# A linear attention with a gated FFN on one core: the last result tiles go to dead operand buffers, and the whole instruction order is rewritten

## The chip, the core and the metric

The kernel runs on one core of a Trainium2 chip. The metric is device time of one execution in microseconds; the kernel before was run three times, with a median of 962.52 us (962.49 to 966.88). One further execution was recorded by the hardware profiler. TensorE does the matrix products, VectorE (DVE) and GpSimd (POOL) do element-wise work, ScalarE (ACT) does activations, copies and some of the DMA issues, and SyncE (SP) issues nearly all other DMAs.

## The reference, cut to what matters

```python
# q, k, v: (8 batches, 8 heads, 576, 64) float32; moe weights float64; 4608 tokens, d_model 512, d_ff 1536
q_s = softmax(q, over the 64 features);  k_s = softmax(k, over the 576 positions)
kv  = einsum('bhsd,bhse->bhde', k_s, v)
x   = einsum('bhsd,bhde->bhse', q_s, kv)          # then 8 heads side by side: 4608 x 512
xn  = x / sqrt(mean(x * x, over the 512) + 1e-6) * rms_g
g   = xn @ w_gate;  val = xn @ w_val              # 512 x 1536 each
out = (g * sigmoid(g) * val) @ w_out              # 1536 x 512, result 4608 x 512 float32
```

## The kernel before

**Data.** The three weights arrive as 8-byte words. `load_w` (L444) brings raw words in by SP, and four steps turn them into float32: `conv_low` (L451) and `conv_mul` (L457) on ACT, `conv_shift` (L460) on DVE, `conv_add` (L465) on POOL. Every matrix operand is then split into a high and a low part, and each product is three matmuls: high by high, high by low, low by high.

**Stages.** Tokens are worked in 9 blocks of 512. The attention part of a block loads q, k and v pieces (SP), takes the maxima and sums of the softmax (DVE), and makes x. Blocks 0 to 2 run the FFN plainly in 12 steps each: `f1` (L973) makes the gate and value products in PSUM, `g_mul` (L978, DVE) scales the gate, `silu` (L982, ACT), `h_mul` (L985, DVE) multiplies, `h_hi` (L408, ACT) and `h_lo` (L994, POOL or DVE) split, and `f2` (L1010) multiplies by w_out. While these run, combinations of the weights are made and kept in DRAM. Blocks 3 to 8 run as three pairs, p = 0, 1, 2. Their first product is a Strassen-Winograd scheme with 7 instead of 8 block products (`pp`, L1122), whose weights come back from DRAM through POOL's queue (`w_in`, L1095, tiles `ring` and `w`); sums of the products are `c_...` (L1143, DVE), and `hm` (L1185, DVE or POOL) multiplies gate and value. The second product is plain for pair 0 and by the same scheme for pairs 1 and 2: `qq` (L1331) multiplies, with weights that SP loads (`qw`), operand parts from `qb_hi` (L408) and `qb_lo` (L1316), and sums on DVE (`q_comb`, L1340) that leave four quadrants, 11, 12, 21 and 22, each in two halves x = 0 and 1.

**The end of the last pair.** For each of these eight halves `qtr` (L1357 to L1360) transposes 32 x 32 pieces on DVE into an `ot` tile, of which there are two (`bufs=2`). For the last pair `qput` (SP) stores the first two 32-row groups of it, and `qpua` (ACT) the other two, each 64 KB by one DMA at L1368. An `ot` tile can be written again when all four stores from it are in. The weights' tiles `w_0` to `w_5`, taken over by the Strassen operands in `operand()` (L1035), are not used again once the last pair's first product is done.

**What sets the order.** Every instruction's place is set by a table, the string `ORDER` (L22): 3345 steps, each the name of a function with its numbers, and after a colon the engine where there is a choice (A, D or P). A loop at L1385 calls them in that order, and each engine executes its own instructions strictly in it. A DMA that SP or ACT issues takes one of eight completion counters in turn, shared by both queues, and its issue waits until the one before it on that counter is in.

Of the kernel before, what the change touches and what calls it, by code (L numbers as in the profile page):

```python
# [8 lines left out]
F32 = mybir.dt.float32  # L9
# [13 lines left out]
exp_table k_load.0.0 q_load0.0.0 kv_zero.4 kv_zero.5 v_ones.0.0 kv_zero.0 k_load.0.2 kv_zero.7 q_load0.0.3 constants  # L23
v_ones.0.1 kv_zero.3 warm.2.3 kv_zero.6 k_max0.0.0 q_load0.0.2 v_ones.0.2 kv_zero0.0 warm.2.10 kv_zero0.1 q_max0.0.0
k_load.0.1 warm.2.1 q_load0.0.1 q_sub0.0.0:P warm.2.6 load_w.0.1 v_ones.0.3 k_max0.0.2 k_load.0.3 q_exp.0.0 warm.2.12
v_load.0.0 k_tr.0.0 warm.2.13 k_top.0.0 q_max0.0.2 k_rows.0.0 load_w.0.2 warm.2.8 k_max0.0.1 k_tr.0.2 warm.2.9
v_load.0.1 q_sub0.0.2:P k_sub.0.0 k_tr.0.1 warm.2.11 warm.2.5 g_load q_max0.0.3 q_exp.0.2 warm.2.7 load_w.0.0 k_top.0.1
q_sub0.0.3:P k_exp.0.0 q_sum0.0.0 k_rows.0.1 warm.9 q_max0.0.1 v_load.0.2 q_exp.0.3 q_eps0.0.0 k_top.0.2 q_sub0.0.1:P
q_rec0.0.0 k_sub.0.1 k_load.1.0 q_mul0.0.0:P q_sum0.0.3 q_exp.0.1 k_exp.0.1 q_sum0.0.1 q_t0.0.0 k_max0.0.3 k_rows.0.2
conv_low.0.2.1 v_load.0.3 k_mm.0.0 conv_low.0.1.1 k_sub.0.2 warm.2.4 q_c0.0.0:A load_w.1.1 k_tr.0.3 warm.2.0  # L30
conv_mul.0.1 q_eps0.0.1 k_eps.0.0 q_eps0.0.3 k_mm.0.1 q_rec0.0.1 k_top.0.3 k_exp.0.2 q_mul0.0.1:P k_rec.0.0 q_sum0.0.2
load_w.1.0 k_rows.0.3 kv_norm0.0.0:A conv_shift.0.1 conv_mul.0.0 q_x0.0.0 q_eps0.0.2 q_rec0.0.3 conv_add.0.1.1
k_eps.0.1 k_sub.0.3 conv_low.0.0.1 q_load0.1.0 q_t0.0.1 conv_mul.0.2 conv_shift.0.0 k_mm.0.2 q_mul0.0.3:P x_hi.0.0:A
k_rec.0.1 conv_shift.0.2 q_c0.0.1:A conv_add.0.0.1 q_rec0.0.2 kv_norm0.0.1:A k_eps.0.2 k_max.1.0 k_exp.0.3 q_x0.0.1
load_w.2.1 q_mul0.0.2:P x_sq.0.0 k_rec.0.2 x_lo.0.0 k_mm.0.3 q_load0.1.1 x_sq.0.1 kv_norm0.0.2:D v_ones.1.0
conv_add.0.2.1 w_hi.0.0.2:A k_tr.1.0 q_t0.0.2 k_eps.0.3 k_top.1.0 k_rec.0.3 x_hi.0.1:D k_rows.1.0 conv_mul.1.1 q_t0.0.3
w_lo.0.0:P warm.2.2 q_c0.0.2:A conv_shift.1.1 kv_norm0.0.3:A q_x0.0.2 x_lo.0.1 kv_zero.2 q_c0.0.3:A load_w.2.0
w_lo.0.1:P k_sub.1.0 conv_mul.1.0 load_w.1.2 q_x0.0.3 x_sq.0.2 v_load.1.0 conv_shift.1.0 n_sum0.0 x_hi.0.2:A q_max0.1.0
x_hi.0.3:A n_sum0.1 x_lo.0.2 q_sub0.1.0:P x_sq.0.3 x_lo.0.3 o_hi.0:A n_sum0.2 q_exp.1.0 q_max0.1.1 o_lo.0:P n_sum0.3
conv_mul.2.1 q_sum0.1.0 conv_low.1.0.2 f1.0.0.0.0 load_w.2.2 conv_shift.2.1 q_sub0.1.1:P f1.0.0.0.1 f1.0.0.0.2  # L40
load_w.4.1 n_t.0 f1.0.0.0.3 conv_mul.2.0 f1.0.1.0.0 load_w.3.1 f1.0.0.1.0 conv_add.1.0.2 f1.0.1.0.1 k_exp.1.0
load_w.4.0 n_y0.0 f1.0.1.0.2 f1.0.1.0.3 conv_shift.2.0 f1.0.0.1.1 conv_low.2.0.2 f1.0.0.1.2 f1.0.0.1.3 n_y1.0
f1.0.1.1.0 load_w.3.0 f1.0.1.1.1 q_exp.1.1 f1.0.1.1.2 f1.0.1.1.3 conv_add.2.0.2 f1.0.0.2.0 w_hi.1.0.2:A f1.0.0.2.1
f1.0.0.2.2 f1.0.0.2.3 q_load0.1.2 k_mm.1.0 n_rows.0 conv_mul.1.2 conv_low.1.2.1 f1.0.1.2.0 g_mul.0 f1.0.1.2.1
f1.0.1.2.2 f1.0.1.2.3 q_eps0.1.0 silu.0 k_eps.1.0 q_rec0.1.0 k_rec.1.0 w_lo.1.0:D f1.1.0 conv_shift.1.2 q_mul0.1.0:P
load_w.6.0 conv_mul.4.1 k_load.1.2 h_mul.0 w_lo.1.1:P w_hi.2.0.2:A kv_norm0.1.0:D f1.1.1 conv_shift.4.1 conv_add.1.2.1
h_hi.0:A load_w.5.0 g_mul.1 conv_mul.4.0 k_load.1.1 conv_mul.3.1 h_lo.0:D o_hi.1:A w_lo.2.0:P conv_shift.4.0 silu.1
f2.0 conv_shift.3.1 load_w.6.1 conv_low.4.0.2 load_w.5.1 h_mul.1 w_lo.2.1:P q_max0.1.2 conv_low.2.2.1 conv_mul.2.2
o_lo.1:D load_w.4.2 conv_mul.3.0 f1.2.0 q_sub0.1.2:P conv_shift.2.2 conv_shift.3.0 conv_mul.6.0 conv_add.4.0.2
load_w.3.2 conv_low.3.0.2 conv_shift.6.0 k_max.1.2 q_load.2.0 q_t0.1.0 f1.2.1 g_mul.2 q_c0.1.0:A conv_add.3.0.2  # L50
q_exp.1.2 k_max.1.1 h_hi.1:A q_sum0.1.2 q_x0.1.0 w_hi.4.0.2:A q_eps0.1.2 h_lo.1:D k_tr.1.1 f2.1 x_hi.1.0:A load_w.5.2
w_lo.4.0:D w_hi.3.0.2:A load_w.8.0 k_top.1.1 q_sum0.1.1 load_w.7.0 silu.2 x_lo.1.0 w_lo.3.1:P load_w.7.1 f1.3.1
v_ones.1.1 q_eps0.1.1 conv_add.2.2.1 q_rec0.1.2 q_rec0.1.1 v_load.1.1 conv_low.6.0.2 h_mul.2 w_lo.3.0:D x_sq.1.0
o_hi.2:A q_mul0.1.2:D k_rows.1.1 conv_mul.6.1 f1.3.0 o_lo.2:P k_sub.1.1 h_hi.2:A conv_shift.6.1 conv_mul.5.0 kv_zero.1
h_lo.2:D conv_low.3.2.1 load_w.6.2 conv_shift.5.0 conv_add.6.0.2 conv_mul.5.1 q_load0.1.3 f2.2 g_mul.3 conv_mul.3.2
conv_shift.5.1 silu.3 conv_shift.3.2 conv_low.4.2.1 q_mul0.1.1:P h_mul.3 conv_mul.7.0 conv_mul.4.2 f1.4.0
conv_shift.7.0 conv_add.3.2.1 h_hi.3:A conv_shift.4.2 conv_low.5.0.2 v_ones.1.2 w_lo.4.1:D load_w.7.2 v_load.1.2
h_lo.3:D o_hi.3:A o_lo.3:P q_t0.1.1 g_mul.4 f1.4.1 q_c0.1.1:A conv_mul.5.2 conv_add.5.0.2 conv_mul.7.1 conv_shift.5.2
silu.4 q_max.2.0 k_exp.1.1 conv_shift.7.1 q_load.2.1 k_tr.1.2 f2.3 conv_add.4.2.1 q_max0.1.3 q_half.2.0 w_hi.5.0.2:A
h_mul.4 k_top.1.2 w_hi.6.0.2:A w_lo.5.1:D k_mm.1.1 w_lo.5.0:D h_hi.4:A k_rows.1.2 f1.5.0 k_eps.1.1 q_max2.2.0  # L60
conv_low.5.2.1 k_rec.1.1 q_sub.2.0:P kv_norm0.1.1:D o_hi.4:A load_w.10.0 load_w.8.1 w_lo.6.1:D q_exp.2.0 load_w.10.1
q_sub0.1.3:P k_sub.1.2 conv_low.7.0.2 load_w.8.2 q_x0.1.1 k_load.1.3 q_sum.2.0 h_lo.4:P k_exp.1.2 g_mul.5 f1.5.1
conv_low.6.2.1 o_lo.4:D x_hi.1.1:A w_lo.6.0:P x_sq.1.1 x_lo.1.1 q_exp.1.3 q_half2.2.0 silu.5 conv_add.7.0.2 k_mm.1.2
q_sum0.1.3 f2.4 k_eps.1.2 conv_mul.7.2 h_mul.5 conv_low.7.2.1 v_ones.1.3 conv_shift.7.2 conv_add.5.2.1 load_w.9.1
h_hi.5:A kv_hi.1.0:D conv_mul.8.1 k_rec.1.2 kv_norm0.1.2:D f1.6.0 conv_add.7.2.1 w_hi.7.0.2:A conv_shift.8.1 o_hi.5:A
q_eps0.1.3 load_w.9.2 conv_low.8.0.2 q_rec0.1.3 h_lo.5:D load_w.9.0 load_w.10.2 w_lo.7.1:D q_t0.1.2 o_lo.5:D f1.6.1
q_c0.1.2:A o_hi.7:D conv_mul.6.2 w_lo.7.0:D conv_low.10.0.2 g_mul.6 o_lo.7:P q_max.2.1 conv_mul.8.2 conv_shift.6.2 f2.5
x_acc.1.1:P silu.6 conv_shift.8.2 conv_mul.8.0 h_mul.6 conv_add.6.2.1 conv_low.8.2.1 conv_shift.8.0 conv_mul.9.0
h_hi.6:A k_max.1.3 conv_add.8.2.1 f1.7.0 conv_mul.9.1 conv_low.9.2.1 q_sum2.2.0 v_ones.2.0 conv_shift.9.0
conv_add.8.0.2 load_w.11.2 o_hi.6:A v_load.1.3 conv_shift.9.1 conv_low.9.0.2 q_rec.2.0 f1.7.1 o_lo.6:D w_hi.8.0.2:A  # L70
h_lo.6:P g_mul.7 w_lo.8.0:D k_tr.1.3 q_x0.1.2 load_w.11.0 conv_add.9.0.2 k_top.1.3 load_w.11.1 q_half.2.1 f2.6
k_load.2.0 x_hi.1.2:A x_sq.1.2 x_lo.1.2 silu.7 conv_mul.10.1 w_lo.8.1:P h_mul.7 k_rows.1.3 h_hi.7:A f1.8.0 q_mul0.1.3:P
k_sub.1.3 w_hi.9.0.2:A q_mul.2.0:D o_hi.8:A q_load.2.2 h_lo.7:P conv_shift.10.1 conv_mul.10.2 conv_mul.10.0 f1.8.1
w_lo.9.0:D k_exp.1.3 w_lo.9.1:P conv_shift.10.2 conv_shift.10.0 g_mul.8 o_lo.8:P conv_mul.9.2 f2.7 conv_low.10.2.1
conv_shift.9.2 v_load.2.0 silu.8 conv_add.10.0.2 n_cols.0 conv_mul.11.0 f1.9.0 conv_add.9.2.1 conv_shift.11.0 q_t.2.0
h_mul.8 kv_hi.1.2:D h_hi.8:A q_t0.1.3 o_hi.9:A k_mm.1.3 h_lo.8:D w_hi.10.0.2:A g_mul.9 o_lo.9:P f1.9.1 k_load.2.1
k_eps.1.3 silu.9 k_rec.1.3 q_c0.1.3:D w_lo.10.0:P kv_hi.1.1:A kv_norm0.1.3:D conv_low.11.2.1 q_load.2.3 conv_mul.11.2
kv_hi.1.3:D x_acc.1.2:P conv_mul.11.1 f1.10.0 conv_shift.11.2 conv_shift.11.1 kv_lo.1.1:P q_max.2.2 conv_add.10.2.1
q_max2.2.1 h_mul.9 q_half.2.2 v_ones.2.1 q_x0.1.3 w_lo.10.1:P f2.8 v_load.2.1 h_hi.9:D g_mul.10 h_lo.9:D silu.10
k_max.2.0 x_sq.1.3 x_hi.1.3:A f1.10.1 o_hi.10:A kv_lo.1.0:D x_acc.1.3:D conv_low.11.0.2 o_lo.10:D conv_add.11.0.2 f2.9  # L80
# [264 lines left out]
def linear_attention_then_gated_ffn(ctx: ExitStack, tc, q, k, v, w_gate, w_val, w_out, rms_g, out):  # L345
    nc = tc.nc
    B, H, S, D = q.shape
    NT, DM = out.shape
# [1004 lines left out]

    def q12(p, x):
        q_comb(p, x, 12, ux[p, "q", x, 2], 2, 2)

    def qtr(p, n, x):  # L1357
        src = qacc[p, 0, x] if n == 11 else ux[p, "q", x, n]
        t = ux[p, "o", x, n] = fp.tile([P, DM], F32, name="ot", bufs=2)
        nc.vector.transpose(t, src)  # L1360
# [57 lines left out]
```

## Time and profile before

| what | before |
|---|---|
| median of 3 runs | 962.52 us (962.49 to 966.88) |
| the profiled execution | 971.66 us, of which its span is 969.9 us |
| TensorE matmul busy | 927.0 us, 96% of the span |
| VectorE busy | 745.6 us, 77% |
| GpSimd busy | 525.1 us, 54% |
| ScalarE busy | 474.7 us, 49% |
| the last matmul ends | 949.71 us after the span's start |

The span is the time from the first to the last instruction that the profiler saw; the execution has 1.8 us around it. In the rows below a time in brackets says how long the engine sat idle before the instruction, and behind the arrow stands what it waited for. PE is TensorE's matrix products, SPq and ACTq are the DMA queues of those engines, and PEclk is the granted TensorE clock as a share of full speed.

### The profile page before, as it was taken

To read this page: it belongs to the slowest core of one execution; us is meant where nothing else is said; L and a number is where in the kernel's file an instruction comes from. 1 tells how busy PE (TensorE), PEld (TensorE's weight loads), DVE (VectorE), ACT (ScalarE), POOL (GpSimd) and SP (SyncE) were. 2 spreads that over 40 slices of the span, in tenths; PEclk is the share of its full clock that TensorE was granted. 3 is DMA by queue.
4 is the path that set the end of the run, shared out by engine and by line. 5 is a ranking of instruction groups with operands and counts; after the bars stand their busy time and mean duration, and the time that the engine had idled before them with its cause. 6 is when DMAs were issued, how large, how long until landed. Compare 5 with 4: busy or idle time off the path is not lost.

```text
span 969.9 us, 14401 instructions
## 1 busy us (share of the span) xinstructions
PE 927.0 (96%) x4625; PEld 750.0 (77%) x4625; DVE 745.6 (77%) x1548; ACT 474.7 (49%) x742; POOL 525.1 (54%) x517
## 2 busy tenths in 40 slices
PE   6999999999999899999999999999999999999991
PEld 4688887777877687887887888888887888888881
DVE  6798868989887789888886698866569855545981
ACT  3999747687577475665534464321216311112320
POOL 4777959767588587774765545333232652412230
PEclk9899999999999999999999999999999999999996
DMA  9997425988976987899788698898538688684334
GB/s 207 279 269 231 137 79 197 303 278 287 320 219 192 254 242 195 207 231 242 197 218 260 220 267 270 272 283 288 169 130 298 155 233 251 216 258 130 109 82 60
DMA packets 215464, 211.80 MB, mean 218 GB/s; under 512 B 139828, under 2 KB 176732, under 8 KB 210780
## 3 DMA queue, kind: packets, MB, share of 16 engines
q1 hardware_dynamic: 190620, 121.73, 45.6%
q0 software_dynamic: 16320, 88.09, 28.8%
q10 hardware_dynamic: 8448, 1.05, 0.7%
q8 instruction: 37, 0.61, 0.3%
q14 instruction: 39, 0.32, 0.1%
HBM read 160.49 MB, written 50.33 MB: 217 GB/s over the span
## 4 chain that ended last, share of the span: by engine, by line
PE 82%; DMA 6%; SPq 5%; DVE 3%; ACT 2%; issue 1%; POOL 0%; ACTq 0%; DVEq 0%; POOLq 0%
PE ps_gv L1122 16%; PE ps_gv L973 15%; PE ps_o L1122 12%; PE ps_o L1010 7%; PE ps_a L1122 7%; PE ps_o L1331 6%; PE ps_a L1331 3%; PE ps_o L1215 3%; PE ps_gv L1331 3%; DMA qt<-in_q_dram 2%; PE ps_a L1215 2%; PE ps_gv L1215 2%; PE ps_a L577 2%; SPq L647 1%; PE ps_a L785 1%; DMA od<-o 1%
## 5 line engine op out<-in xcount | busy, mean ns | idle before, releaser
L973 PE MATMUL ps_gv<-xh,w 128*128 128x512 f32 x576 | 191.8, 400 | 6.3 <-DVE gs L978 5.0
L1122 PE MATMUL ps_gv<-x,ring 128*128 128x512 f32 x576 | 142.7, 392 | 0.0
L973 PEld LDWEIGHTS ps_gv<-xh,w 128*128 128x128 f32 x576 | 108.8, 189 | 32.5 <-DVE gs L978 5.8
L1122 PEld LDWEIGHTS ps_gv<-x,ring 128*128 128x128 f32 x576 | 107.1, 188 | 22.8 <-DVE tmp L1143 0.3
L973 PE MATMUL ps_gv<-xl,w 128*128 128x512 f32 x288 | 112.1, 393 | 0.0
L1143 DVE TENSOR_TENSOR tmp<-tmp,ps_gv 128x512 f32<-128x512 f32 x84 | 57.3, 685 | 41.4 <-PE ps_gv L1122 40.5
L1122 PE MATMUL ps_o<-x,ring 128*128 128x512 f32 x360 | 85.0, 389 | 0.0
L1095 POOL DMA_DIRECT2D ring<-wd x54 | 30.9, 573 | 93.4 <-PE ps_gv L1122 43.2
L1122 PEld LDWEIGHTS ps_o<-x,ring 128*128 128x128 f32 x360 | 67.5, 188 | 14.3 <-DVE tmp L1143 0.2
L1010 PE MATMUL ps_o<-o,hh 128*128 128x512 f32 x288 | 73.8, 398 | 2.5 <-ACT hh L408 2.5
L897 POOL TENSOR_TENSOR w<-w,w 128x512 fp32r<-128x512 f32 x43 | 61.0, 1426 | 11.5 <-ACT w L408 11.5
L1010 PEld LDWEIGHTS ps_o<-o,hh 128*128 128x128 f32 x288 | 52.8, 188 | 15.1 <-ACT hh L408 3.7
L973 PEld LDWEIGHTS ps_gv<-xl,w 128*128 128x128 f32 x288 | 54.4, 189 | 10.5 <-issue 0.2
L1143 DVE TENSOR_TENSOR tmp<-tmp,ps_o 128x512 f32<-128x512 f32 x42 | 28.7, 684 | 21.0 <-PE ps_o L1122 20.4
L1095 POOL DMA_DIRECT2D w<-wd x18 | 10.0, 556 | 58.3 <-PE ps_a L1122 29.1
L408 ACT CAST hh<-gs 128x512 fp32r<-128x512 f32 x48 | 29.5, 616 | 23.6 <-DVE gs L985 8.8
L534 DVE TENSOR_REDUCE cm<-kt 116x128 f32<-116x640 f32 x28 | 36.6, 1306 | 4.4 <-DMA kt<-in_k_dram 4.3
L1010 PE MATMUL ps_o<-o,hl 128*128 128x512 f32 x144 | 38.7, 391 | 0.0
L994 POOL TENSOR_TENSOR hl<-gs,hh 128x512 fp32r<-128x512 f32 x23 | 32.8, 1425 | 10.4 <-ACT hh L408 8.0
L1122 PE MATMUL ps_a<-x,ring 128*128 128x512 f32 x144 | 37.1, 393 | 0.1
L1122 PE MATMUL ps_a<-x,w 128*128 128x512 f32 x144 | 36.8, 391 | 0.0
L1122 PE MATMUL ps_gv<-x,w 128*128 128x512 f32 x144 | 35.5, 392 | 0.3 <-DVE w L1143 0.3
(620 smaller groups left out, 2312.1 us busy)
## 6 DMA issues: line engine op xcount, KB each, us to landing
ring<-wd POOLq DMA_DIRECT2D x36, 768.0 KB, 5.9
w<-wd POOLq DMA_DIRECT2D x24, 1024.0 KB, 6.0
ring<-wd POOLq DMA_DIRECT2D x18, 1024.0 KB, 6.0
wd<-w SPq DMA_DIRECT2D x12, 1024.0 KB
wd<-parts SPq DMA_DIRECT2D x24, 512.0 KB
o<-od POOLq DMA_DIRECT2D x18, 512.0 KB, 5.7
kt<-in_k_dram SPq DMA_DIRECT2D x28, 280.0 KB
vt<-in_v_dram SPq DMA_DIRECT2D x56, 140.0 KB
```

The lines of the kernel that those rows point to most:

```text
L408: (e.copy if e is nc.scalar else e.tensor_copy)(dst, src)
L534: nc.vector.tensor_reduce(out=cm, in_=kt_[b, g].rearrange("p h j d -> p h d j"), axis=AX.X, op=ALU.max)
L577: nc.tensor.matmul(pk[h * D:(h + 1) * D, :D + 1], lhsT=ke[:n, h, j], rhs=vt[:n, j, h], start=(j == 0), stop=(j == len(rows) - 1))
L897: on(nc.gpsimd).tensor_tensor(out=w[:, :, 1], in0=halves(s % NF, a, 1)[:, 0], in1=w[:, :, 0].bitcast(F32), op=ALU.subtract)
L973: nc.tensor.matmul(pd[s], lhsT=w[:, a, c // 2, m, c % 2 * P:c % 2 * P + P], rhs=X[j, c][x], start=(n == 1), stop=(n == 3 * NKT))
L994: on(nc.gpsimd).tensor_tensor(out=hl, in0=g_[s], in1=h_[s][0].bitcast(F32), op=ALU.subtract)
L1010: nc.tensor.matmul(po[t], lhsT=a[:, t * P:(t + 1) * P], rhs=w, start=(i == 0 and n == 0), stop=(i == NF - 1 and n == len(terms) - 1))
L1095: nc.gpsimd.dma_start(t, src.rearrange("p a b f -> p (a b f)"))
L1122: nc.tensor.matmul(abc[p, i, m, b], lhsT=src[:, h, c * P:(c + 1) * P], rhs=operand(o, c, x), start=first and n == 0, stop=n == 5, skip_gro ...
L1143: nc.vector.tensor_tensor(out=dst, in0=ux[u + (src,)], in1=abc[u + (b,)], op=ALU.add)
L1215: nc.tensor.matmul(pa[p, t, k], lhsT=a[:, k * P:(k + 1) * P], rhs=w, start=(c == 0 and n == 0), stop=(c == NF - 1 and n == 2))
L1331: nc.tensor.matmul(qacc[p, b, x], lhsT=ws[l][x], rhs=h[m], start=first and i == 0 and n == 0, stop=i == NH - 1 and n == 2, skip_group_chec ...
```

## The change

The last pair's transposed halves no longer go to the two `ot` tiles. Each half gets a slice of its own in two tiles that take the places `w_0` and `w_1`:

```diff
+    RES = {}
+
     def qtr(p, n, x):
         src = qacc[p, 0, x] if n == 11 else ux[p, "q", x, n]
-        t = ux[p, "o", x, n] = fp.tile([P, DM], F32, name="ot", bufs=2)
+        if p == NPAIR - 1:
+            m = (11, 22, 21, 12).index(n) * 2 + x
+            if m // 6 not in RES:
+                RES[m // 6] = big.tile([P, 6, TB], F32, name=f"res_{m // 6}", tag=f"w_{m // 6}")
+            t = RES[m // 6][:, m % 6]
+        else:
+            t = fp.tile([P, DM], F32, name="ot", bufs=2)
+        ux[p, "o", x, n] = t
         nc.vector.transpose(t, src)
```

And the whole of `ORDER` is another order of the same 3345 steps, with other engines for some of them. Its last lines before and after:

```diff
-... qq.2.3.5 qq.2.2.4.0 qq.2.2.5.0 qq.2.2.4.1 qq.2.2.5.1 qtr.2.11.1 q12.2.0 qput.2.11.1
-qpua.2.11.1 qput.2.21.0 qtr.2.12.0 qpua.2.12.0 qtr.2.11.0 q12.2.1 qput.2.11.0 qpua.2.11.0 ...
+qq.2.3.3 qb_lo.2.3.5:D qq.2.3.4.0 qq.2.3.5.0 qq.2.3.4.1 q12.2.0 qq.2.3.5.1 qtr.2.12.0 q12.2.1 qput.2.12.0 qpua.2.12.0
+qtr.2.12.1 qput.2.12.1 qpua.2.12.1
```

The numbers of matmuls (4249), of transposes (62) and of DMAs from SP (747) and POOL (108) stay. Two-input element-wise instructions go from 696 to 675 on DVE and from 348 to 369 on POOL; `hm` stands on POOL 30 times instead of 18. Table loads on ACT go from 58 to 52, and the step that loads the exponential's table at the very start now stands late in the order. Lines after the change are one higher near the top, and 10 higher behind `qtr`.

**The end, on DVE.** The last rows before; `tmp` and `gs` hold quadrant sums, `ps_o` and `ps_a` are PSUM banks, and a number tells tiles of one name apart.

```order
L1340 TENSOR_TENSOR tmp_4494<-tmp_4494,ps_o_8282 128x512
L1316 TENSOR_TENSOR hl_6794<-w_5834,hh_6793 128x512
L1316 TENSOR_TENSOR kv_102<-kt_7553,kv_102 128x512
L1360 STREAM_TRANSPOSE ot_9117<-ps_o_8203 128x512
L1340 TENSOR_TENSOR gs_8902<-gs_8902,ps_a_8817 128x512
L1360 STREAM_TRANSPOSE ot_9126<-gs_8902 128x512
L1360 STREAM_TRANSPOSE ot_9130<-ps_o_8202 128x512
L1340 TENSOR_TENSOR gs_8897<-gs_8897,ps_a_8818 128x512
L1360 STREAM_TRANSPOSE ot_9137<-gs_8897 128x512
L1360 STREAM_TRANSPOSE ot_9143<-tmp_4494 128x512
```

And the last rows after, with the tiles `res_0` and `res_1`.

```order
L1341 TENSOR_TENSOR tmp_4478<-tmp_4478,ps_o_8278 128x512
L1370 STREAM_TRANSPOSE res_0_9006<-tmp_4478 128x512
L1341 TENSOR_TENSOR tmp_4478<-tmp_4478,ps_o_8279 128x512
L1370 STREAM_TRANSPOSE res_0_9006<-tmp_4478 128x512
L1317 TENSOR_TENSOR vt_7112<-w_5828,kt_7111 128x512
L1317 TENSOR_TENSOR kv_102<-w_5828,kv_102 128x512
L1341 TENSOR_TENSOR gs_8902<-gs_8902,ps_a_8813 128x512
L1370 STREAM_TRANSPOSE res_1_9133<-gs_8902 128x512
L1341 TENSOR_TENSOR gs_8889<-gs_8889,ps_a_8814 128x512
L1370 STREAM_TRANSPOSE res_1_9133<-gs_8889 128x512
```

Five transposes stood behind the last operand part (L1316) and now two do; the other six halves are transposed before it.

**The first loads, on SP.** Before, from the third row of the queue (one k piece and two q halves stand ahead); `w_94` and `w_95` hold v and k pieces, `qt` and `r` q halves, `raw` weight words.

```order
L494 DMA w_95<-in_k_dram 96x2x384
L661 DMA r<-in_q_dram 128x256 x2
L661 DMA qt<-in_q_dram 128x256 x2
L494 DMA w_95<-in_k_dram 96x2x384
L661 DMA qt<-in_q_dram 128x256 x2
L444 DMA raw_98<-in_moe_w_val_dram 128x4x256
L494 DMA w_95<-in_k_dram 96x2x384
L519 DMA w_94<-in_v_dram 96x6x64 x2
L444 DMA raw_98<-in_moe_w_out_dram 128x1024
L519 DMA w_94<-in_v_dram 96x6x64 x2
L434 DMA g_sb<-in_moe_rms_g_dram 128x4x1
L444 DMA raw_98<-in_moe_w_gate_dram 128x4x256
```

After, from the start of the queue.

```order
L495 DMA w_95<-in_k_dram 96x2x384 x3
L662 DMA qt<-in_q_dram 128x256 x4
L495 DMA w_95<-in_k_dram 96x2x384
L662 DMA qt<-in_q_dram 128x256 x2
L445 DMA raw_99<-in_moe_w_val_dram 128x4x256
L445 DMA raw_98<-in_moe_w_val_dram 128x4x256
L520 DMA w_94<-in_v_dram 96x6x64 x2
L662 DMA r<-in_q_dram 128x256 x2
L445 DMA raw_98<-in_moe_w_gate_dram 128x4x256
L520 DMA w_94<-in_v_dram 96x6x64 x4
L520 DMA w_93<-in_v_dram 96x6x64 x2
L435 DMA g_sb<-in_moe_rms_g_dram 128x4x1
```

The first gate words stood behind one val tile, the w_out tile, two pairs of v pieces and the small `g_sb`; now they stand behind two val tiles and one pair of v pieces.

**Block 2's last steps, on DVE.** Before, the rows around the gate scaling of step 29 (`g_mul.29`, the L978 row): `st` tiles are the maxima of q pieces of block 5, `st_3745` from the piece whose load is `q_load.5.1`, `st_3752` from that of `q_load.5.0`.

```order
L713 TENSOR_REDUCE st_3745<-qt_3634 128x16
L718 TENSOR_REDUCE st_3745<-st_3745 32x16 x4
L713 TENSOR_REDUCE st_3752<-qt_3560 128x16
L718 TENSOR_REDUCE st_3752<-st_3752 32x16 x4
L726 TENSOR_REDUCE sw_3772<-st_3752 128x16
L597 TENSOR_SCALAR rs_3774<-ps_a_3758 128x1
L565 TENSOR_TENSOR kt_3290<-kt_3290,ps_a_3725 116x640
L978 TENSOR_TENSOR gs_3794<-ps_gv_3685,r_2777 128x512
```

After, the same place: `st_3756` is the maximum of the piece of `q_load.5.0`, `st_3776` that of `q_load.5.1`.

```order
L566 TENSOR_TENSOR kt_3502<-kt_3502,ps_a_3707 116x640
L714 TENSOR_REDUCE st_3756<-qt_3524 128x16
L979 TENSOR_TENSOR gs_3758<-ps_gv_3709,r_2897 128x512
L765 STREAM_TRANSPOSE qT_3761<-qt_3376 128x512
L714 TENSOR_REDUCE st_3776<-qt_3664 128x16
L775 TENSOR_TENSOR ql_3790<-qT_3647,qh_3684 128x512
```

Before, both maxima stood ahead of the gate scaling; after, only that of the earlier loaded piece does.

## Rows read from the trace of the kernel before

**Rows 1.** The page: span, TensorE's busy time, the chain by engine.
```profile
span 969.9 us, 14401 instructions
...
PE 927.0 (96%) x4625; PEld 750.0 (77%) x4625; DVE 745.6 (77%) x1548; ACT 474.7 (49%) x742; POOL 525.1 (54%) x517
...
PE 82%; DMA 6%; SPq 5%; DVE 3%; ACT 2%; issue 1%; POOL 0%; ACTq 0%; DVEq 0%; POOLq 0%
```

**Rows 2.** Timeline, 943 to 970 us: start, length, engine, line, operation [idle before].
```profile
948.85 0.86 PE L1331 MATMUL ps_o<-kv,x 128*128 128x512 f32 x3
949.75 0.72 DVE L1360 STREAM_TRANSPOSE ot<-ps_o 128x512 f32<-128x512 f32 x1 [4.33 <-PE ps_o L1331]
950.38 0.65 DVE L1340 TENSOR_TENSOR gs<-gs,ps_a 128x512 f32<-128x512 f32 x1
950.49 16.05 SPq L1368 DMA_DIRECT2D out_dram<-ot  x12
...
963.56 0.71 DVE L1360 STREAM_TRANSPOSE ot<-tmp 128x512 f32<-128x512 f32 x1 [3.61 <-DMA out_dram<-ot]
```

**Rows 3.** Chain that ended last, 938 to 970 us: start, length, what.
```profile
950.50 0.38 ACTq L1368
...
950.91 3.02 DMA out_dram<-ot
...
960.39 2.94 DMA out_dram<-ot
```

**Rows 4.** Waits of DVE and PE: total us, times, longest.
```profile
DVE ot L1360 <- DMA out_dram<-ot: 9.8, 3, 3.6
...
PE ps_gv L973 <- DVE gs L978: 5.0, 3, 4.3
```

**Rows 5.** Busy time by stretch, with clock, DMA share, GB/s.
```profile
20.00:30.00 10.00, 7.45 (x58) 4.29 (x58) 5.14 (x14) 7.77 (x16) 6.29 (x7) 0.68 1.05 218
...
333.10:337.50 4.40, 4.37 (x12) 3.49 (x13) 3.86 (x11) 3.82 (x7) 4.35 (x6) 0.62 0.67 154
800.00:900.00 100.00, 100.00 (x442) 82.58 (x441) 53.70 (x82) 19.04 (x34) 25.88 (x29) 1.00 0.67 208
920.00:940.00 20.00, 20.00 (x88) 16.31 (x87) 17.36 (x30) 6.52 (x11) 4.08 (x3) 1.00 0.36 87
...
949.80:969.90 20.10, 0.00 (x0) 0.00 (x0) 4.66 (x7) 0.00 (x0) 0.00 (x0) 0.55 0.52 72
```

**Rows 6.** Chain that ended last, 8 to 45 us.
```profile
15.21 9.38 DMA raw<-in_moe_w_gate_dram
...
28.22 2.08 PE ps_o L707 x2
...
39.73 4.56 PE ps_gv L973 x20
```

**Rows 7.** Timeline, ACT: the first table load; the first gate words.
```profile
0.73 1.28 ACT L475 ACT_TABLE_LOAD   x1 [0.73 <-PEq L1403]
...
24.62 0.63 ACT L457 ACTIVATE ps_a<-raw 128x512 f32<-128x512 f32 x1 [1.76 <-DMA raw<-in_moe_w_gate_dram]
```

**Rows 8.** Timeline, 316 to 334 us: block 2's last steps.
```profile
316.22 12.53 SPq L647 DMA_DIRECT2D qt<-in_q_dram  x16
...
328.64 0.69 DVE L713 TENSOR_REDUCE st<-qt 128x16 f32<-128x512 f32 x1 [6.07 <-DMA qt<-in_q_dram]
...
332.39 0.68 DVE L978 TENSOR_TENSOR gs<-ps_gv,r 128x512 f32<-128x512 f32 x1
333.13 0.50 PE L973 MATMUL ps_gv<-xh,w 128*128 128x512 f32 x1 [4.30 <-DVE gs L978]
```

**Rows 9.** Groups by line and form: count, busy us, mean ns, idle before.
```profile
L994 POOL TENSOR_TENSOR hl<-gs,hh 128x512 fp32r<-128x512 f32 x23 | 32.8, 1425 | 10.4 <-ACT hh L408 8.0 <-DVE hh L408 2.4
L994 DVE TENSOR_TENSOR hl<-gs,hh 128x512 fp32r<-128x512 f32 x13 | 10.1, 774 | 1.5 <-ACT hh L408 1.5
L759 DVE TENSOR_TENSOR qt<-qt,sm 128x512 f32<-128x512 f32 x7 | 9.7, 1387 | 0.1
```

## What the change was predicted to do

> **What bounds the kernel now.** The page comes first: TensorE is busy for 927.0 of 969.9 us, and it carries 82% of the chain that ended last; DMA and SP's queue follow with 6% and 5% [rows 1]. So time can be won only where TensorE stands still, at three kinds of place. The last is the largest. In the timeline the last matmul ends at 948.85 + 0.86 = 949.71 us, and the span goes on to 969.9: 20.2 us, 2.1% of all, in which DVE does seven instructions, 4.66 us [rows 2, 5]. The chain shows what fills them: a store from an `ot` tile lands after about 3 us, then the next transpose begins, and this repeats [rows 3]. The waits sum it: DVE's transposes wait three times, 9.8 us, for stores to leave the two tiles [rows 4]. The second place is ahead of 949.71: 949.7 - 927.0 = 22.7 us of TensorE's idleness, part of it in the front end, where the windows show 7.45 busy of 10 us at 20 to 30 us, at a granted clock of 0.68 [rows 5], and where the chain passes through the load of the first gate words [rows 6]. The third is one stall at 328.8 to 333.1 us, the longest wait of TensorE for the gate scaling [rows 4, 8].
>
> **The tail.** What leaves is the waiting for the two tiles, and, by the new order, six of the eight transposes and their stores from behind the last matmul. Let T be its end. One matmul takes 100.00 / 442 = 0.226 us [rows 5]. In the new order the six matmuls of half x = 1 come last, so half x = 0 of the last quadrant is complete at T - 6 x 0.226 = T - 1.36; its sum (0.65) and transpose (0.71, [rows 2]) end at about T + 0.04. The sum of x = 1 begins 0.04 after T (949.71 to 949.75) and is transposed by T + 0.04 + 0.65 + 0.71 = T + 1.40. From the end of the last transpose before, 963.56 + 0.71 = 964.27, to the end of the span are 5.6 us; so the end would come at T + 7.0.
>
> A second path is the stores' own. ACT's last store shares its completion counter with SP's first store of the half x = 0. That one is issued at about T + 0.04 in 0.38, lands 2.94 later [rows 3], then ACT issues in 0.38, lands in 2.94, and 0.5 are left to the span's end: T + 7.2. I take this later one: 20.2 - 7.2 = 13.0 saved. Bounds: with no shared counter in the way 20.2 - 7.0 = 13.2; if the stores jam, four halves of 256 KB (those of the last two quadrants) at the 72 GB/s of the tail [rows 5] need 14.2 us from T - 5 on, so the end is at T + 9.2 + 0.5, and 10.5 are saved. Cover: the six early transposes and their sums now stand on DVE while TensorE multiplies. The last 14 `qq` steps give 14 x 1.36 = 19 us of TensorE, and DVE has 21 instructions in them, at most 0.79 each by the nearest form, 0.774 [rows 9]: 16.6. That fits, if narrowly; DVE was just as full before, 17.36 of 20 us, with TensorE at 20.00 of 20.00 [rows 5]. So it costs nothing; if that cover fails, about one instruction too late, 0.8, is lost.
>
> **The front.** The first gate words are awaited at 24.6 us [rows 7], and in the chain their load takes 9.38 us and sets TensorE's work from 28.22 on [rows 6]. Ahead of this load SP's queue held 3778 KB (four k pieces of 288 KB, eight q halves of 128, four v pieces of 144, the val and w_out tiles of 512 each), and holds 3488 KB now (a second val tile instead of w_out, two v pieces fewer): 0.29 MB less, at 218 GB/s [rows 5] 1.3 us sooner. Against that, ACT has by the new order about 3 us more of conversions and copies between the gate words and the last input of the first f1, one of them with 1024 columns, at twice the 0.63 of a 512 one [rows 7]; a part of them runs while it waits anyway. The two sides nearly cancel. I take -0.5 us, with bounds of -3 (all of the waiting for the gate words, 1.76, and the load's gain) and +2 (ACT's extra work, bare). The table load that moves from the start, 1.28 us at 0.73 [rows 7], ran while ACT had nothing else; now the same table is loaded at the first exponential, for whose input ACT waits anyway: nothing, or 1.28 if that input is there.
>
> **The stall at 333 us.** Before the gate scaling of step 29 DVE had two maxima of q pieces of block 5, and waited 6.07 us for the first of them, whose pieces SP had been issuing since 316.22 [rows 8]. TensorE waited 4.30 us, and was then granted 0.62 of its clock: its next 12 matmuls took 4.37 instead of 12 x 0.226 = 2.71 us [rows 5]. Together 4.3 + 1.7 = 6.0. In the new order the later loaded piece's maximum stands behind the gate scaling, and the other's load lies farther ahead. All of 6.0 can go. But a profiled execution is 9.1 us longer than the median of the ordinary ones, 971.66 against 962.52, and such a wait for a DMA may be part of that; and 3345 steps in another order can put another DVE row behind a late load somewhere else. I take half, -3.0, with bounds of -6.0 and +3, half such a stall more.
>
> **Element work moved to POOL.** 21 two-input instructions go from DVE to POOL, 12 of them `hm`. On DVE the nearest form takes 0.774, on POOL 1.425 [rows 9]. DVE has 46 us free in 100 in the pair stage and POOL 74, while TensorE is at 100.00 [rows 5]; so it costs and gives nothing, as long as nobody waits for the longer instruction. Gain if DVE's time counted: 21 x 0.774 = 16 us; loss if POOL's did, 21 x 1.425 = 30 us. Zero is nearest to what TensorE shows.
>
> The trace has a sign that the two engines hinder each other: `L759` on DVE, both inputs in SBUF, takes 1.387, nearly twice the 0.774 of `L994` [rows 9]. The Trainium skill, page SBUF — State Buffer, section SBUF: two separate sides, says that a DVE instruction with two SBUF inputs and a GpSimd one take turns at a shared port pair, the later one fully blocked. By that rule part of the relief on DVE would be given back, up to 1.4 us for each pair that meets; by the row alone, 0.6. Since the relief is counted at nothing, the sum is the same by either as long as TensorE is covered; where it is not, the rule speaks for the slower rival below.
>
> **The sum.** -13.0 - 0.5 - 3.0 = -16.5 us. On the profiled execution's own time, 971.66 - 16.5 = 955.2; taken from the median, 962.52 - 16.5 = 946.0. Six fewer table loads at 1.28 [rows 7] are ACT's, which is busy for 49% [rows 1], and count nothing.
>
> **The rivals.**
> - Only the tail counts: the new order puts as many waits on TensorE as it removes. Then 962.5 - 13.0 = 949.5, or with one more stall like that at 333 us 955. For it speaks that nearly every step has moved; against it that the tightest loads stand farther ahead of their use in the new order.
> - More of the idleness goes: a third of the 18.4 us that are left of 22.7 besides the 4.3. That gives 946 - 6 = 940. The same loads speak for it, the front against it.
> - The tiles aren't what holds the end: TensorE's last work could now outrun DVE, or the stores queue on the counters and the DMA engines. The jam above leaves 10.5; if half the eight halves still stood behind the last matmul, with stores of 3.6 us each, 20.2 - 4 x 3.6 - 1.4 - 0.5 = 4 are saved: 958. The 16 DMA engines' share of 0.52 in the tail [rows 5] speaks against it.
> - Slower: the 12 `hm` and 9 others on POOL delay the weight loads that POOL itself issues behind them and the operands that TensorE waits for. If all 21 reach TensorE at 1.425 each, the time is 946 + 30 = 976. It decides from 12 of them on (16.5 / 1.425), beyond the half per cent from 15 on. TensorE's 100.00 of 100 us with POOL busy for 25.88 [rows 5] speaks against it.
>
> **How the numbers follow.** Forecast 946 (its own range 941 to 951), 55%; tail alone 949.5 to 956, 25%; more idleness gone, 938 to 941, 9%; stores still late, 953 to 958, 6%; POOL on the path, 963 to 976, 5%. The range of 938 to 956 leaves out the last case, most of the fourth and a little at either end of the others. Half a per cent, 4.8 us, is what a measurement can tell from no change: faster means under 957.7, slower over 967.3. The cases give 0.88, 0.08 and 0.04.
>
> **What would show it.** Right: some 7 us between the last matmul and the end, no transposes waiting for stores, two transposes behind T; no wait of the gate scaling near 330 us; the first f1 within a microsecond or two of where it was. Wrong: a chain that ends in stores from 958 us on; a new row of waits of TensorE for DVE or POOL in the middle of the run, above all `hm` ahead of a weight load in the pair stage; a granted clock under 1 in windows where before it was 1.00.

## The result and the profile after

The changed kernel takes 954.52 us, median of 6 runs (953.01 to 958.68); the kernel before took 965.2, median of 6 (962.49 to 968.16). The ratio is 0.9895, 95% interval 0.9864 to 0.9925. Run again beside other kernels it was 955.66 against 967.94: 0.9871 (0.9843 to 0.9900). So it is faster, by 10.7 us in the first set and 12.3 in the second; the two intervals together leave 7 to 15 us open. The forecast of 946 us had the sign and the place; the gain was two thirds to three quarters of the 16.5 us forecast.

The first lines of the page after, beside [rows 1]:

```profile
span 951.7 us, 14402 instructions
...
PE 925.5 (97%) x4625; PEld 748.1 (79%) x4625; DVE 739.0 (78%) x1516; ACT 469.3 (49%) x747; POOL 553.3 (58%) x538
```

TensorE works as long as before; 18.2 us of span have gone from around it. The timeline of the end, beside [rows 2] (start, length, engine, line, operation, idle before):

```profile
938.27 9.50 ACTq L1378 DMA_DIRECT2D out_dram<-res  x8
...
943.70 0.69 DVE L1341 TENSOR_TENSOR gs<-gs,ps_a 128x512 f32<-128x512 f32 x1 [2.97 <-PE ps_a L1332]
...
944.20 0.86 PE L1332 MATMUL ps_a<-kv,x 128*128 128x512 f32 x3
944.43 0.71 DVE L1370 STREAM_TRANSPOSE res<-gs 128x512 f32<-128x512 f32 x1
945.09 0.69 DVE L1341 TENSOR_TENSOR gs<-gs,ps_a 128x512 f32<-128x512 f32 x1
945.81 0.71 DVE L1370 STREAM_TRANSPOSE res<-gs 128x512 f32<-128x512 f32 x1
```

Six of the 3345 steps are not the same as before: there the products `qq.2.2.4` and `qq.2.2.5` come in halves, here `qq.2.3.4` and `qq.2.3.5`, so that half x = 0 of the last quadrant is complete six matmuls before the end. The last matmul ends at 944.20 + 0.86 = 945.06, the span 6.6 us later instead of 20.2. No transpose waits for a store, the half x = 0 is transposed by 945.14 while its partner is still summed, and the last transpose ends 1.46 us behind the last matmul. The chain up to the last transpose has no store in it any more; 5.2 us, in which the last stores are issued and land, follow it:

```profile
936.74 6.94 PE ps_a L1332 x30
943.68 0.02 issue
943.70 0.70 DVE gs L1341
944.40 0.02 issue
944.43 0.71 DVE res L1370
945.14 0.65 DVE gs L1341
945.79 0.02 issue
945.81 0.71 DVE res L1370
```

The windows of the front and of the end (us, busy of PE, PEld, DVE, ACT, POOL, clock, DMA share, GB/s), beside [rows 5]:

```profile
20.00:30.00 10.00, 7.14 (x89) 4.49 (x86) 7.86 (x23) 9.02 (x18) 7.38 (x7) 1.00 1.09 304
30.00:40.00 10.00, 9.93 (x38) 6.69 (x37) 9.33 (x25) 8.38 (x14) 7.86 (x6) 1.00 1.10 304
945.10:951.70 6.60, 0.00 (x0) 0.00 (x0) 1.39 (x3) 0.00 (x0) 0.00 (x0) 0.66 0.58 80
```

In this pair of traces the clock in the front is 1.00 where it was 0.68. And the longest waits of TensorE (total us, times, longest), beside [rows 4], no longer name the gate scaling. A wait like the first stands in before too, at 2.8 us; the two for sums of L1144 are new:

```profile
PE ps_gv L471 <- POOL mean_w L432: 2.2, 1, 2.2
PE ps_gv L1123 <- DVE tmp L1144: 1.8, 1, 1.8
PE ps_o L1011 <- ACT ot L414: 1.6, 2, 1.2
...
PE ps_o L1123 <- DVE tmp L1144: 1.1, 1, 1.1
```

Put together from the first two traces: the first f1 starts at 34.96 instead of 39.17 (-4.2), from there to the last matmul's end it takes 910.1 instead of 910.5 (-0.4), and the end is 6.6 instead of 20.2 (-13.6): -18.2. But the medians differ by 10.7 only. The first trace of before was 971.66 us, above all six timed runs of it (later ones reached 975.17), and the runs below show which of the three terms belong to the kernel and which to that one execution.

### The profile page after: what moved, and what is told of

It is laid out like the page before. It is cut to its first block, busy times and chain, and to the rows that moved or that the text cites. A ratio compares the mean times of both kernels' runs of the same rounds, so it can differ in the third digit from the quotient of the medians.

```text
span 951.7 us, 14402 instructions
## 1 busy us (share of the span) xinstructions
PE 925.5 (97%) x4625; PEld 748.1 (79%) x4625; DVE 739.0 (78%) x1516; ACT 469.3 (49%) x747; POOL 553.3 (58%) x538
## 3 DMA queue, kind: packets, MB, share of 16 engines
q10 hardware_dynamic: 8448, 1.05, 0.7%
## 4 chain that ended last, share of the span: by engine, by line
PE 76%; DMA 8%; DVE 7%; SPq 3%; issue 3%; ACT 2%; POOL 1%; DVEq 0%; POOLq 0%; ACTq 0%
PE ps_gv L1123 16%; PE ps_gv L974 12%; PE ps_o L1123 12%; PE ps_o L1011 6%; PE ps_o L1332 6%; PE ps_a L1123 6%; PE ps_a L1332 3%; PE ps_o L1216 3%; PE ps_gv L1332 3%; DMA qt<-in_q_dram 2%; SPq L648 2%; DMA kt<-in_k_dram 2%; PE ps_a L1216 2%; PE ps_gv L1216 2%; PE ps_a L578 1%
## 5 line engine op out<-in xcount | busy, mean ns | idle before, releaser
L974 PE MATMUL ps_gv<-xh,w 128*128 128x512 f32 x576 | 189.8, 398 | 2.8 <-DVE gs L986 1.2
L1144 DVE TENSOR_TENSOR tmp<-tmp,ps_gv 128x512 f32<-128x512 f32 x84 | 57.2, 682 | 52.9 <-PE ps_gv L1123 52.0
L1144 DVE TENSOR_TENSOR tmp<-tmp,ps_o 128x512 f32<-128x512 f32 x42 | 28.4, 684 | 31.8 <-PE ps_o L1123 30.7
L898 POOL TENSOR_TENSOR w<-w,w 128x512 fp32r<-128x512 f32 x31 | 44.0, 1427 | 11.8 <-ACT w L409 8.3
L906 POOL TENSOR_TENSOR o<-w,o 128x512 fp32r<-128x512 f32 x22 | 29.4, 1338 | 23.6 <-ACT o L409 8.2
L1011 PE MATMUL ps_o<-o,hl 128*128 128x512 f32 x144 | 39.2, 394 | 1.9 <-DVE hl L995 1.4
L535 DVE TENSOR_REDUCE cm<-kt 116x128 f32<-116x640 f32 x28 | 36.8, 1316 | 0.7 <-DMA kt<-in_k_dram 0.4
L409 ACT COPY tmp<-ps_a 128x512 f32<-128x512 f32 x22 | 12.8, 586 | 49.0 <-PE ps_a L1123 48.9
L1123 PE MATMUL ps_gv<-x,w 128*128 128x512 f32 x144 | 35.2, 391 | 0.0
```

Source lines behind the costliest of these rows:

```text
L409: (e.copy if e is nc.scalar else e.tensor_copy)(dst, src)
L535: nc.vector.tensor_reduce(out=cm, in_=kt_[b, g].rearrange("p h j d -> p h d j"), axis=AX.X, op=ALU.max)
L898: on(nc.gpsimd).tensor_tensor(out=w[:, :, 1], in0=halves(s % NF, a, 1)[:, 0], in1=w[:, :, 0].bitcast(F32), op=ALU.subtract)
L906: on(nc.vector).tensor_tensor(out=ol, in0=W(s % NF, 2), in1=oh.bitcast(F32), op=ALU.subtract)
L974: nc.tensor.matmul(pd[s], lhsT=w[:, a, c // 2, m, c % 2 * P:c % 2 * P + P], rhs=X[j, c][x], start=(n == 1), stop=(n == 3 * NKT))
L1011: nc.tensor.matmul(po[t], lhsT=a[:, t * P:(t + 1) * P], rhs=w, start=(i == 0 and n == 0), stop=(i == NF - 1 and n == len(terms) - 1))
```

## The experiments

In each, three numbers are read from the trace: the start of the first f1, the time from there to the end of the last matmul, and the tail from there to the end of the span. Before has 39.2, 910.5 and 20.2; after has 35.0, 910.1 and 6.6.

**The tiles alone.** After's `qtr` with before's `ORDER`.

> The order of before, with only the result tiles changed: each half of the last pair goes to a slice of its own. Theory (the two tiles hold the end): the transposes wait for no store; seven DVE instructions, 4.8 us, then 5.6 us as before to the end, so 10.4 instead of 20.2 us behind the last matmul, and the time is 9.8 us (1.0%) below before; the half per cent left to the version after is its front and its order. Rival (the order alone gives the end): five halves stay behind the last matmul, and their 20 stores of 64 KB at the tail's 72 GB/s need 18 us, so the tail stays at 18 to 20 us and the time within 2 us of before.

Measured: 960.32 against 967.31, ratio 0.9940 (0.9914 to 0.9967). First f1 36.8, then 906.5, tail 957.1 - 943.32 = 13.8. Neither number of the expectation: the tail lost 6.4 us, not 9.8. The timeline of its end:

```profile
942.46 0.86 PE L1334 MATMUL ps_o<-kv,x 128*128 128x512 f32 x3
943.36 0.72 DVE L1372 STREAM_TRANSPOSE res<-ps_o 128x512 f32<-128x512 f32 x1 [4.33 <-PE ps_o L1334]
...
944.11 9.68 SPq L1380 DMA_DIRECT2D out_dram<-res  x12
944.11 7.88 ACTq L1380 DMA_DIRECT2D out_dram<-res  x10
...
947.24 0.67 DVE L1372 STREAM_TRANSPOSE res<-tmp 128x512 f32<-128x512 f32 x1
```

DVE is done at 947.91, 4.6 us behind the last matmul, as worked out; no transpose waits. What is late next are the stores. From 944.11 on 22 of them are issued, for five halves and SP's part of a sixth. SP's twelve issues take until 953.79, one every 0.8 us on average, though the first takes 0.32, and the end comes 3.3 us behind the last of them. Over these stores the 16 DMA engines are busy without a break; the last three numbers are the granted clock, the DMA share and GB/s:

```profile
944.90:955.30 10.40, 0.00 (x0) 0.00 (x0) 2.97 (x5) 0.00 (x0) 0.00 (x0) 0.54 1.00 140
```

The tail of before had a share of 0.52 and 72 GB/s [rows 5]. So with the tiles' wait gone, 22 stores in a row set the end. Which part of their path holds them is not shown: the DMA engines are full, but 13 of the 14 stores behind the first eight are also issued within 0.08 us of the landing of the store before on their completion counter.

**The order alone.** After's `ORDER`, and two slots in rotation for the eight halves, as the two `ot` tiles were.

```diff
-            m = (11, 22, 21, 12).index(n) * 2 + x
+            m = turn["res"] = (turn.get("res", -1) + 1) % 2
```

> The order of after, with two slots in rotation for the last pair's halves instead of eight. Theory: halves come to the transposes 1.4 to 3 us apart while a slot is blocked for about 4 us, so transposes wait again, and operand parts that DVE makes behind them reach TensorE late: 3 to 9 us slower than after, TensorE idle in the last 30 us and a tail of 9 to 13 us. Rival (the order alone): within 1 us of after, tail 6.6 us.

Measured: 956.76 against 967.31, ratio 0.9907 (0.9872 to 0.9942); 35.2, 909.5, tail 6.7. In this kernel half 11.1 is written over half 11.0 before ACT has stored its part, so it leaves out some of the waiting that two slots need. It was repeated with that store one step earlier (in `ORDER`, `qpua.2.11.0` ahead of `qtr.2.11.1`):

> The order of after with two slots in rotation, and ACT's store of half 11.0 moved one step ahead, so that each slot is stored before it is written again; the whole result is computed. If the two slots still matter in the new order: transposes wait for stores during the last 25 us, DVE's later operand parts are late, and the last matmul and the end are 2 to 6 us later than in after. If the order alone took their weight away: the same time as after within 1 us, a tail of 6.6 us, no transposes waiting more than 1 us.

Measured: 957.13 against 967.94, ratio 0.9885 (0.9855 to 0.9915); 34.9, 910.8, tail 952.3 - 945.61 = 6.7. Transposes do wait again, a little (total us, times, longest):

```profile
DVE res L1371 <- DMA out_dram<-res: 2.4, 2, 1.4
```

TensorE covers it: its only wait from 915 us on is one of 0.3 us. So the tail of 6.6 us is the order's: with halves finished one after another under the matmuls, even two slots would do. The new tiles are worth 6.4 us in the old order, and nothing that can be measured in the new one. What they give the new order is freedom, by its steps and not by a run: with two `ot` tiles and its order word for word, the transpose of half 11.1 would wait for ACT's store of 11.0, which ACT has queued behind its store of 11.1.

**The fronts exchanged.** The first 260 steps of after ahead of the rest of before, and the reverse.

```diff
-exp_table k_load.0.0 q_load0.0.0 kv_zero.4 kv_zero.5 ...
+k_load.0.0 k_load.0.1 kv_zero.0 kv_zero.4 k_load.0.2 ...
```

> The order of before, with the first 260 steps (the front and the first two f1 steps) in the order of after; the end as before. Theory (the front of after is worth what its trace shows, 4 us): the first f1 starts at about 35 us instead of 39.2, no granted clock under 1.00 between 20 and 40 us, tail 20 us, time 4 us below before. Rival (the earlier start is given back to later conversions and loads in blocks 0 to 2): f1 at 35 us, but time within 1 us of before.

> The order and tiles of after, with the first 260 steps in the order of before. Theory: 4 us slower than after (first f1 at 39 us), 6.5 us of tail. Rival: within 1 us of after, since the wait for converted weights in the first steps comes anyway.

Measured: 968.11 against 967.31, ratio 1.0021 (0.9998 to 1.0044), and 957.75 against 967.31, ratio 0.9914 (0.9883 to 0.9945), where after had 0.9895 and 0.9871. The first f1 starts at 37.3 with the new front and at 35.4 with the old one, against both theories. Each joint also makes waits of its own between 40 and 60 us (18.0 and 16.2 us of TensorE in 20). As a price of the front the two are inconclusive; what they showed is that the order of the front alone does not set its start.

**The same program again.** Before and after, unchanged.

> The kernel before once more, for a second trace of it. Theory: the stall of TensorE at 333 us (4 to 6 us with the lower clock behind it) and the tail of 20.2 us are there again, since they belong to the order; the first f1 starts at 34 to 38 us instead of 39.2, since its start differs from execution to execution, and the time is 3 to 6 us under the 971.66 of the first trace. Rival: the first f1 is at 39 again, as the order of the first loads sets it, and the stall was an accident of the first trace.

> The kernel after once more, on the chip of the runs beside it: 10 to 11 us below before, tail 6.6 us. Its trace is the second one of the same program: stalls that stand in both belong to the order, those in one of them to the execution.

Measured: 964.77 for before (one run; 968.10 beside it), with 34.3, 908.5 and a tail of 20.2; 955.66 for after, with 38.0, 908.9 and 6.6. The second trace of before, its last matmuls and the maximum at DVE whose wait was 6.07 us in [rows 8]:

```profile
span 963.0 us, 14401 instructions
```

```profile
321.69 0.69 DVE L716 TENSOR_REDUCE st<-qt 128x16 f32<-128x512 f32 x1 [3.63 <-DMA qt<-in_q_dram]
...
941.96 0.86 PE L1334 MATMUL ps_o<-kv,x 128*128 128x512 f32 x3
```

TensorE's waits for the gate scaling in this trace (total us, times, longest), beside the 5.0 and 4.3 of [rows 4]:

```profile
PE ps_gv L976 <- DVE gs L981: 2.6, 3, 1.9
```

With before's front the first f1 started at 39.2, 36.8, 35.4, 35.4, 34.3, 33.8 and 33.8 us in the seven traces that have it, mean 35.5; with after's at 35.0, 38.0, 37.3, 35.2, 34.9, 35.3 and 35.2, mean 35.8. The 4.2 us of the first pair of traces are the execution's, and no difference between the fronts shows against this spread. The start goes with the granted clock ahead of it: from 10 to 33.8 us it was 1.00 in nine of these traces, of both fronts, which start at 33.8 to 35.4, and 0.78 to 0.93 in the five others, which start at 33.8 to 39.2. DVE's wait for the q piece near 333 us is the order's: it stands in all five traces that have before's order there (6.07, 3.63, 1.90, 6.62 and 5.21 us). What reaches TensorE is the execution's: 4.30, 1.91, 0.24, 4.85 and 3.45 us of stall in the same traces, the 0.24 in that of the tiles alone.

**The stall at 333 us.** Before, with the later q piece's maximum behind the gate scaling.

```diff
-q_max.5.1 q_half.5.1 o_lo.28:P q_max.5.0 ... g_mul.29 o_lo.29:P
+o_lo.28:P q_max.5.0 ... g_mul.29 q_max.5.1 q_half.5.1 o_lo.29:P
```

> The order of before, with two steps moved: the maximum of the q piece of q_load.5.1 and its half stand behind the gate scaling of step 29 instead of ahead of it. Theory (a wait that only some executions have): the stall at 333 us is gone, and the time is 1 to 3 us below before on average, less than the 6.0 of the first trace. Rival (every execution has it): 6 us below before. Third: the other maximum, of q_load.5.0, waits in its place, and nothing changes.

Measured: 963.46 against 967.94, ratio 0.9952 (0.9930 to 0.9974): -4.5 us. First f1 35.4, then 905.2. Its waits of TensorE for the gate scaling, against 5.0 us in [rows 4]:

```profile
PE ps_gv L976 <- DVE gs L981: 0.9, 3, 0.5
```

So the wait costs 4.5 us on average (2.5 to 6.8 by the interval), more than the 1 to 3 of the first theory; 6.0 is not excluded. The change removed it too and should have had these 4.5 us, yet it took 910 us for that stretch.

**The end alone, and the end with that one edit.** Before's first 2888 steps, then after's end; and the same with the two steps moved. The seam lies at 777 us of the trace, in the first of the six groups of the last pair's first product, and not behind most of that product, as the first expectation has it. From the seam to the last matmul TensorE shows no wait in before, in after or in the end alone, so only the tail differs there.

```diff
 ... (before's order up to the last pair's first product)
-... qq.2.2.5.1 qtr.2.11.1 q12.2.0 qput.2.11.1 ...
+... qq.2.3.5.1 qtr.2.12.0 q12.2.1 qput.2.12.0 qpua.2.12.0 qtr.2.12.1 qput.2.12.1 qpua.2.12.1
```

> The order of before in its first 2888 steps (all of the front, blocks 0 to 2, pairs 0 and 1, and most of the last pair's first product), then the order and tiles of after: the end alone. Theory (the end is the whole gain, and the other reordering gives nothing or loses 2 to 3 us in ordinary runs): tail 6.6 us, time 13.5 us below before, so 2 to 3 us below after. Rival (front and middle of after gain what the two first traces show, 4 to 5 us): tail 6.6 us and time 3 to 5 us above after.

> The order of before in its first 2888 steps with the two steps of the maximum of q_load.5.1 behind the gate scaling of step 29, then the end of after. Theory: both gains add, 12 to 13.5 us of the end and 3 to 6 of the stall, so 15 to 18 us below before and 4 to 6 below after; no stall of TensorE over 2 us between 60 and 940 us. Rival (another late load takes the stall's place): within 2 us of the end alone, 12 to 13.5 below before.

Measured: 954.74 against 967.94, ratio 0.9839 (0.9807 to 0.9872), tail 7.0, and after beside it 955.66: the end alone gives all that the change gives, if not a little more, which the intervals leave open. And 947.82 (947.03 to 950.16) against 965.07, ratio 0.9812 (0.9766 to 0.9859), tail 6.6: faster than both kernels. The end alone had drawn the stall in full; with two steps moved it is gone. DVE's wait for that load, first in the timeline of the end alone, then TensorE's wait for the gate scaling with both edits:

```profile
325.34 0.69 DVE L716 TENSOR_REDUCE st<-qt 128x16 f32<-128x512 f32 x1 [6.62 <-DMA qt<-in_q_dram]
```

```profile
PE ps_gv L976 <- DVE gs L981: 0.9, 3, 0.5
```

From the first f1 to the last matmul it was 912.0 with the stall, 905.1 without. In all six traces with the old order up to the seam this stretch follows the stall: 905.1 and 905.2 with the edit, 906.5 with a stall of 0.24, 908.5 with 1.91, 910.5 with 4.30, 912.0 with 4.85.

**Where the new order loses.** All four traces with the new order unchanged (two of after, two with two slots) show a wait of TensorE of 1.8 us at 390 us, and one of 1.05 at 609; no trace of the old order has either. In the second trace of after:

```profile
387.38 1.31 POOL L775 TENSOR_TENSOR ql<-qT,qh 128x512 fp32r<-128x512 f32 x1
387.50 4.21 DVE L731 TENSOR_TENSOR qt<-qt,sw 128x512 f32<-128x512 f32 x1
...
388.63 1.29 POOL L1079 TENSOR_TENSOR x<-xh,x 128x512 fp32r<-128x512 f32 x1
...
389.88 1.27 POOL L995 TENSOR_TENSOR hl<-gs,hh 128x512 fp32r<-128x512 f32 x1
...
391.63 0.68 DVE L1144 TENSOR_TENSOR tmp<-tmp,ps_gv 128x512 f32<-128x512 f32 x1
...
392.36 1.69 PE L1123 MATMUL ps_gv<-x,ring 128*128 128x512 f32 x6 [1.82 <-DVE tmp L1144]
```

A subtraction (`q_sub.6.2`) of a line that takes 0.67 to 1.02 us elsewhere on DVE takes 4.21 beside three POOL instructions in a row, here and in four other traces, and the sum that TensorE waits for stands behind it. Its shape is not the cause: in after's first trace the 175 DVE instructions of this kind, both inputs in SBUF and no two-input POOL instruction beside them, took 0.69 us at most. The test gives this one step to POOL:

```diff
-q_sub.6.2:D
+q_sub.6.2:P
```

> After, with one step on another engine: the subtraction q_sub.6.2, which on DVE took 4.21 us beside three POOL instructions in a row, goes to POOL behind them. Theory (it is held by POOL, and all of DVE's queue with it): the 1.8 us wait of TensorE for a sum of L1144 at 390 us and the lower clock behind it go, DVE has no instruction over 3.2 us there, and the time is 1 to 3 us below after. Rival (the instruction is slow by its own shape, or the late operands of the next steps set the time): within 1 us of after.

Measured: 954.47 against 965.07, ratio 0.9885 (0.9839 to 0.9931). The same window (387.50 to 391.70 and on) of after's second trace, then of this kernel:

```profile
387.50:391.70 4.20, 3.04 (x31) 2.23 (x29) 4.20 (x2) 0.13 (x1) 4.19 (x5) 1.00 0.81 254
391.70:395.00 3.30, 2.64 (x9) 2.18 (x10) 3.06 (x13) 3.22 (x5) 1.29 (x1) 0.83 0.88 272
```

```profile
387.50:391.70 4.20, 4.20 (x30) 3.25 (x30) 2.77 (x9) 3.14 (x7) 3.96 (x5) 1.00 0.75 196
391.70:395.00 3.30, 3.30 (x29) 2.72 (x26) 3.01 (x13) 2.13 (x4) 3.28 (x5) 1.00 0.70 247
```

The stall is gone, 1.8 us of it there and the lower clock behind it. In the whole time it can't be seen: from the first f1 to the last matmul it is 909.7, against 910.1 and 908.9. This trace has another wait of TensorE instead, at 290 us, with a granted clock of 0.86 in the 10 us behind it, where after's two traces have 1.00:

```profile
PE ps_o L1012 <- ACT ot L415: 2.5, 1, 2.5
```

That this instruction makes the stall at 390 us is shown; what the stall costs in the whole time is not measured.

**Work on POOL.** After, with `hm` on the engines of before.

```diff
-hm.2.4.21:P ... hm.2.4.22:D ...   (20 steps: 16 from POOL to DVE, 4 the other way)
+hm.2.4.21:D ... hm.2.4.22:P ...
```

> After, with the gate-value products hm on the engines that they had before (20 of them change: 12 fewer on POOL in sum). If work moved to POOL costs and gives nothing there: within 1 us of after, TensorE at 100 of 100 us in the pair stages. If POOL's longer instructions are on the path: 1 to 5 us below after. If DVE's relief was needed: 1 to 5 us above, with TensorE waiting for DVE sums from 600 us on.

Measured: 958.40 against 965.07, ratio 0.9911 (0.9879 to 0.9944), where after had 0.9871 and 0.9895; not told apart. Its trace has 98.95 of 100 us of TensorE between 600 and 700, exactly what after has there, where before had 100.00: the wait at 609 us does not come from `hm`'s engines. So the 12 more products on POOL are not what that order loses. If anything they help: the stretch from the first f1 to the last matmul is 913.2 here, against 908.9 to 910.8 in the four traces of the new order, and the median leans the same way, but the intervals leave zero open.

## Why the prediction was right and too large

- **The tail: right.** 13.0 forecast, 13.6 measured. The last transpose ended 1.46 us behind the last matmul, where 1.40 was worked out, and 5.2 us followed instead of 5.6. The later path, over the shared counter, which the forecast took, did not hold the end: ACT's last issue was over at 938.27 + 9.50 = 947.77, 2.7 us behind the last matmul, and not 3.7. The working named the order as the cause for six of eight halves, and the runs bear it out further: it is the order's, and the tiles alone give 6.4.
- **DVE's cover at the end: right.** No transpose or operand part delays TensorE in the last 20 us: from 926 us to its last matmul TensorE is busy for 19.06 of 19.06 us, while DVE does 23 instructions in 15.15, where the working had 21 in 16.6.
- **The front: right in size, for a reason not shown.** -0.5 was forecast; the means of seven traces each differ by 0.3 us, the other way, in a spread of 5. The first two traces alone would have said -4.2, which also would have been wrong.
- **The stall at 333 us: the failed step.** "All of 6.0 can go ... I take half." The wait went, and it is worth 4.5 us by itself. But the order put others in its place: the stretch from the first f1 to the last matmul took 909.8 on average in the four traces of the unchanged new order (910.1, 908.9, 909.5 and 910.8), and 909.4 in four of the old with the maximum ahead of the scaling (910.5, 908.5, 906.5 and 912.0). So the term of -3.0 came out at 0, give or take the 2 or 3 us that these traces scatter by. What took its place are the 1.8 us at 390 us, the 1.05 at 609, and one stretch of lower clock in each trace (0.83 from 388 to 398 us in after's two, 0.86 from 284 to 296 in those with two slots). The sum had no term for new waits; only the bound of +3 spoke of them. This is the rival "only the tail counts", which had 25%: the result lies in the stated range through it, and outside the forecast's own 941 to 951.
- **The base.** 962.52 was the median of three runs; the six runs of the result have 965.2, and 25, 13 and 17 later ones 967.31, 967.94 and 965.07. So 955.2, the sum on the profiled execution's own time, came out nearer by chance than 946.0. Of the miss of 8.5 us, 2.7 are the base and 3.5 the two terms that gave nothing; the tail gave 0.6 more than forecast, and the last 2.9 are inside the interval.
- **POOL's extra work: 0 is not refuted.** With `hm` moved back the time was the same within the intervals, if anything longer. But TensorE was not covered everywhere in the middle, and there the two engines did hinder each other: the DVE subtraction of 4.21 us ends 0.56 behind the last of the three POOL instructions beside it. The rule of the Trainium skill (SBUF — State Buffer, SBUF: two separate sides), that one of two such instructions is blocked until the other ends, agrees with this, and the row adds that three POOL instructions in a row hold a single DVE instruction through all three.

## What to carry to other kernels

When a wait for a buffer ends a kernel, work out what is late next before pricing its removal: here 22 stores in a row took over half of the gain, and finishing the results one by one under the last matmuls gave the whole of it, with or without more buffers. One trace mixes what the program sets with what that execution drew; a stall counts as the program's when two traces of it have it, and its price comes from runs without it: the same late load held TensorE for 0.24 us in one trace and 4.85 in another. And when a whole order is rewritten, keep the part that pays and put it on the old order: two edits to the order of before came out at 947.8, below both.

## What the runs showed of the hardware

One element-wise DVE instruction with two inputs in SBUF took 4.20 to 4.21 us beside three POOL instructions back to back, in five traces of five, where its kind took 0.69 at most without them. With 22 stores of 64 KB in a row the 16 DMA engines showed a share of 1.00 at 140 GB/s, and SP's issues took 0.32 to 0.91 us, median 0.68. The start of the first large product moved over 5 us, from 33.8 to 39.2, between traces with one order of the front; with a granted clock of 1.00 from 10 to 33.8 us it lay between 33.8 and 35.4.
